# Attention and a low-rank mixer MLP on one core: token tiles in a shared ring of eight, and the preparation of batch 2 moved to the end of batch 0

## The chip, the cores and the metric

The kernel runs on one core of a Trainium2 chip. The metric is device time in microseconds (us) for one execution. PE is the matrix engine, PEld its weight loads; DVE, ACT and POOL are the vector, scalar and GpSimd engines; SP is the queue from which most DMAs are issued. Each engine executes its own instructions in program order and waits on semaphores for the others.

## What is computed

For 8 batches of 12 heads, 448 tokens and head width 64, in fp32 outside and bf16 inside the chip:

```python
q_n, k_n = rmsnorm(q, g_q), rmsnorm(k, g_k)          # over the head width
attn = softmax(q_n @ k_n.T / 8)                      # per head
x = (attn @ v), heads side by side                   # (8, 448, 768)
u = x + (U @ V mixing over the 448 tokens)           # rank 32
out = u + relu(u @ w_ch1) @ w_ch2                    # 768 -> 3072 -> 768
```

## The kernel before

**Units of work.** A batch has three *loads* t of four heads each (t = 0..23) and six *pairs* p of two heads each (p = 0..47). Load 6 and pair 12 are the first of batch 2. For each load, q and k arrive in fp32 by a DMA on SP (`load`, halves s = 0 for k and 1 for q), v by another (`load_v`). The preparation of a load is `squares` (ACT for t < 2 and t > 5, POOL otherwise), `reduce` (DVE), `rsqrt` (two ACT instructions), `scale` (DVE, two multiplies for each of the two pairs), `yield_port` (a 1x1 POOL copy that makes POOL wait for DVE) and `cast_v` (POOL). The squares of loads from 4 on share a single buffer (line 221, `bufs=1`), so the squares of q cannot start before the sums of k have been taken. `transposes` (L250) turns a pair's q and k around on PE for pairs below 14, and by a DMA on SP above; the two copies out of PSUM and, for the DMA form, `gains` are on DVE. Then come `scores` (PE), `expo` (ACT) and `values` (PE, followed by three DVE instructions: L302 the reciprocal, L303 the three whole token tiles, L306 the shared half tile).

**Token tiles.** 448 tokens are 3.5 tiles of 128. An even batch has three whole tiles and a half one, the odd batch after it a half one and three whole ones; the two halves share one tile of 128 rows. Before the change the whole tiles of a batch are one buffer `x3` of a pool of two, and the shared tiles are two constants `xss` that are set to zero at the start (L129 and L130). The second of them is also the operand of `heat` (L759), matmuls at the start whose result nobody reads.

**Order.** The program order is written out by hand. `head` (L591) does batch 0's attention and its low-rank mixing. Then, for each batch b, the matmuls of its MLP (`mlp`, L482) are the filling, and `weave` (L743) puts pieces of other work between them: the attention of batch b+1 and then its mixing. `mlp` yields after every six matmuls; I call these six a *group*. For batch 0 there are 44 groups: 20 of the first layer (L488, hidden blocks 4 to 23) and 24 of the second (L413, six products `po` of four groups each, every one followed by a DVE addition L506 and a store on SP). `weave` spreads items by their weights over a share of the volume: the attention of batch 1 over a share of 0.66 (FA0), the mixing of batch 1 over 0.09 (FM); the last quarter of batch 0 then runs without anything between. An item of weight 0 follows directly on the one before it.

**What is prepared when.** Loads run two ahead: during pairs 8 to 11 SP issues loads 6 and 7, and ACT, DVE and POOL prepare load 6 and half of load 7, so that batch 2's attention finds its first pair ready when batch 1's MLP begins. The second weight, `w2b`, is loaded by six DMAs on POOL's queue: the first ahead of pair 6, one after each of the pairs 6 to 10 (`late`).

**PSUM.** `ps_mm` has three buffers, used in turn by the MLP products, by the transposes, and by some of the values and mixing products; a product can only start when the buffer that it gets has been read out.

Of the kernel before, what the change touches and what calls it, by code (L numbers as in the profile page):

```python
# [17 lines left out]
def kernel(  # L18
# [45 lines left out]
    xpool = ctx.enter_context(tc.tile_pool(name="xpool", bufs=2))  # L64
# [26 lines left out]
    FA, FM, NPE, FA0 = (0.74, 0.77), 0.09, 14, 0.66  # L91
# [20 lines left out]
    def E_of(p):  # L112
        return Es[p % 3 if p < 6 else p % 2]
# [4 lines left out]
    xss = [consts.tile([P, dm], BF16, name=f"xs{i}") for i in range(2)]  # L118

    def setup():  # L120
        nc.scalar.preload_act_table_set("natural_log_exp_and_others")
        make_identity(nc, ident)
        nc.gpsimd.memset(eps, D * 1e-6)
        for t in vas:
            nc.gpsimd.memset(t[:, :, :, D:D + 1], 1.0)
        for t in Es:
            nc.gpsimd.memset(t[:, :, 0:PAD], 0.0)
            nc.gpsimd.memset(t[:, :, PAD + NJ * S:], 0.0)
        for t in xss:  # L129
            nc.gpsimd.memset(t, 0.0)  # L130
        nc.gpsimd.memset(UT, 0.0)
        nc.gpsimd.memset(Vsh, 0.0)
        nc.gpsimd.memset(one, 1.0)
        for i, g in enumerate((g_q, g_k)):
            nc.scalar.dma_start(grow[:, i], g.rearrange("(o a d) -> o a d", o=1, a=1).to_broadcast([1, 2, D]))
# [42 lines left out]

    def load_w2(half, i):
        c, d = slice(8 * i, 8 * (i + 1)), slice(half * HALF, (half + 1) * HALF)  # L180
        nc.gpsimd.dma_start(w2b[:, c, d], w2r[:, c, d])
# [3 lines left out]
    qks, vts, sqs, rstds, qkns, qkTs, scs, x3_of = {}, {}, {}, {}, {}, {}, {}, {}  # L185
# [95 lines left out]
    def values(p, hh):  # L281
        b = p // 6
        par = b % 2
        if b not in x3_of:
            x3_of[b] = xpool.tile([P, 3, dm], BF16, tag="x3", name="x3")
        x3, xs, E, va = x3_of[b], xss[(b // 2) % 2], E_of(p), va_of(p // 2)
        t0, sh, rows = (0, 3, slice(0, 64)) if par == 0 else (1, 0, slice(64, 128))
        hl = 2 * (p % 2) + hh
        d0 = (2 * (p % 6) + hh) * D
        if hh and p < 6:  # L290
            o = ps_mm.tile([P, 4, D + 1], FP32, tag="mm")
        elif hh and p % 6 == 5:
            o = ps_s.tile([P, 4, D + 1], FP32, tag="s", name="o")
        else:
            o = ps_o.tile([P, 4, D + 1], FP32, tag="o")
        for i, off in enumerate(OFFS[par]):
            for kc in range(NJ):
                c = PAD + kc * S + off
                nc.tensor.matmul(o[:, i, :], E[:, hh, c:c + P], va[:, hl, kc, :],  # L299
                                 start=(kc == 0), stop=(kc == NJ - 1))  # L300
        rec = attn.tile([P, 4], FP32, tag="rec")
        nc.vector.reciprocal(rec, o[:, :, D])  # L302
        nc.vector.tensor_tensor(x3[:, :, d0:d0 + D], o[:, t0:t0 + 3, 0:D],  # L303
                                rec[:, t0:t0 + 3].rearrange("p c -> p c ()").to_broadcast([P, 3, D]),
                                OP.mult)
        nc.vector.tensor_tensor(xs[rows, d0:d0 + D], o[rows, sh, 0:D],  # L306
                                rec[rows, sh:sh + 1].to_broadcast([64, D]), OP.mult)
# [4 lines left out]
    def x_tiles(b):  # L312
        xs = xss[(b // 2) % 2]
        full = [x3_of[b][:, i, :] for i in range(3)]
        return full + [xs] if b % 2 == 0 else [xs] + full
# [200 lines left out]
    def attention(b, extra={}):  # L516
# [3 lines left out]
        def add(weight, fn, *args):  # L520
            items.append((weight, lambda: fn(*args)))
# [9 lines left out]
        for p in range(b * 6, b * 6 + 6):  # L531
# [10 lines left out]
            if not odd and p > 7 and t + 2 < NT:  # L542
                add(0, load, t + 2, 1, (0,))
# [15 lines left out]
            if odd and p > 6 and 6 <= t + 2 < NT:  # L559
                add(0, load, t + 2, 1, (1,))  # L560
# [22 lines left out]
            if odd and p > 6 and 6 <= t + 2 < NT:  # L583
                add(0, load_v, t + 2)
            if p in extra:
                add(0, *extra[p])
        add(2, values, b * 6 + 5, 0)
# [128 lines left out]
    scratch = consts.tile([1, 1], BF16, name="scratch")  # L716

    def yield_port(t, pr):

        nc.gpsimd.tensor_copy(scratch, qkns[2 * t + pr][0:1, 1, 0, 0, 0:1])  # L720

# [33 lines left out]
    def heat(n):  # L755
        if n:
            warm = ps_mm.tile([P, 512], FP32, tag="mm")
            for _ in range(n):
                nc.tensor.matmul(warm, xss[1][:, 0:P], xss[1][:, 0:512], start=True, stop=True)  # L759
# [5 lines left out]
    with tc.manual_schedule():  # L765
        head()
        late = {6 + i: (load_w2, *divmod(i + 1, 3)) for i in range(5)}
        for b in range(B):
            fill, total = mlp(b), volume(b)
            if b + 1 < B:  # L770
                rest = [(4, lambda: (load_w2(0, 0), transposes(6), reduce(4, ALL, (0,))))] + attention(1, late)
                weave(fill, total * (FA[b % 2] if b else FA0), attention(b + 1) if b else rest)
                weave(fill, total * FM, mixing(b + 1))
            for _ in fill:
                pass
# [30 lines left out]
```

The softmax here doesn't subtract the row's maximum and nothing guards it: scores larger than these inputs give would overflow.

## Time and profile before

| | us |
|---|---|
| median of 4 runs | 580.17 (578.74 to 580.99) |
| the profiled execution | 579.44 |
| its span, first to last instruction | 577.7 |
| PE busy | 560.3 (97%) |
| DVE busy | 396.6 (69%) |
| ACT busy | 279.9 (48%) |
| POOL busy | 77.6 (13%) |
| DVE L303, three whole tiles, 128x192, 96 times | 34.3 busy, 0.357 each |
| DVE L306, the half tile, 64x64, 96 times | 20.8 busy, 0.217 each |

An engine's busy time is the union of its instructions' spans. PE at 97% does the work that sets the end almost everywhere; so the places of interest are those where PE stands still, and the instructions whose movement can open or close such a place. A wait in a timeline stands in square brackets behind the instruction that waited: how long its engine was idle and what ended it.

### The profile page before, as it was taken

The numbers are of one execution on the slowest core, as the hardware profiler recorded it, in microseconds if no ns is written. First come the engines' busy times: TensorE is split into PE (matmuls) and PEld (weight loads), VectorE is DVE, ScalarE is ACT, GpSimd is POOL, SyncE is SP. The second block draws the span as 40 slices with busy tenths as digits, with TensorE's granted clock in tenths as the row PEclk, the third lists the DMA queues.
The fourth block names the chain that finished last, engine by engine and source line by source line (L and its number), as shares of the span: only waits on it lengthen the run. The fifth ranks groups of instructions, "written<-read, shape, count | busy, mean of one in ns | idle before, by whom it ended". The sixth has DMA issues, their size and how long they took to land.

```text
span 577.7 us, 11342 instructions
## 1 busy us (share of the span) xinstructions
PE 560.3 (97%) x4590; PEld 306.1 (53%) x4613; DVE 396.6 (69%) x811; ACT 279.9 (48%) x413; POOL 77.6 (13%) x122
## 2 busy tenths in 40 slices
PE   7799999999999999999999999999999999999997
PEld 2365556544565555544465555544456555554464
DVE  5878987399875787747776598747767487453342
ACT  4956662266721775166641676246661376302200
POOL 4751421000020000000020000000001000000010
PEclk9999999999999999999999999999999999999999
DMA  8999997524463455444525454456234541040021
GB/s 211 232 241 237 234 172 163 125 56 91 115 133 97 116 131 129 107 104 112 129 74 117 106 128 113 121 143 129 64 84 130 131 97 33 29 110 0 1 54 56
DMA packets 103648, 67.22 MB, mean 116 GB/s; under 512 B 54716, under 2 KB 102060, under 8 KB 103596
## 3 DMA queue, kind: packets, MB, share of 16 engines
q1 hardware_dynamic: 93988, 56.77, 41.6%
q0 software_dynamic: 9376, 9.44, 10.0%
q8 instruction: 36, 0.59, 0.4%
q10 hardware_dynamic: 232, 0.30, 0.2%
q14 instruction: 16, 0.13, 0.1%
HBM read 52.19 MB, written 11.01 MB: 109 GB/s over the span
## 4 chain that ended last, share of the span: by engine, by line
PE 86%; DVE 7%; ACT 3%; DMA 2%; issue 1%; POOL 1%; DVEq 0%; POOLq 0%; ACTq 0%
PE ph L488 35%; PE pb L413 10%; PE po L413 8%; PE o L299 7%; PE pe L413 7%; PE sc L273 7%; PE pa L413 6%; ACT E L278 2%; DVE qkn L244 2%; PE pu L337 2%; PE warm L759 1%; DMA qkT<-qkn 1%; DVE rstd L231 1%; PE first L732 1%; DVE hT L404 1%
## 5 line engine op out<-in xcount | busy, mean ns | idle before, releaser
L488 PE MATMUL ph<-u,w1b 128*128 128x384 bf16 (+1 forms) x1107 | 231.0, 353 | 1.4
L278 ACT ACTIVATE E<-sc 112x896 bf16<-112x896 f32 x184 | 159.9, 914 | 58.0 <-PE sc L273 57.1
L488 PEld LDWEIGHTS <-w1b 128*128 128x128 bf16 x1128 | 102.8, 98 | 108.6 <-issue 22.4
L413 PEld LDWEIGHTS <-hT 128*128 128x128 bf16 x1080 | 101.3, 98 | 71.5 <-issue 9.2
L491 ACT ACTIVATE hT<-ph 128x384 bf16<-128x384 f32 (+1 forms) x95 | 51.4, 543 | 136.2 <-PE ph L488 134.4
L493 DVE TENSOR_SCALAR hT<-ph 128x512 bf16<-128x512 f32 (+1 forms) x93 | 57.8, 622 | 53.6 <-PE ph L488 52.9
L299 PEld LDWEIGHTS <-E 112*128 112x128 bf16 x1472 | 58.5, 98 | 15.9 <-DVE xs L306 1.6
L244 DVE TENSOR_TENSOR qkn<-qk,rstd 112x512 bf16<-112x512 f32 x84 | 56.2, 706 | 7.9 <-ACT rstd L237 4.1
L299 PE MATMUL o<-va,E 112*128 112x65 bf16 x1440 | 61.0, 194 | 0.5 <-DVE xs L306 0.5
L273 PE MATMUL sc<-qkT 64*128 64x448 bf16 x384 | 55.5, 355 | 3.5 <-ACT E L278 1.4
L413 PE MATMUL po<-w2b,hT 128*128 128x384 bf16 x288 | 52.5, 326 | 0.6 <-DVE hT L493 0.6
L231 DVE TENSOR_REDUCE rstd<-sq 112x16 f32<-112x1024 f32 x40 | 48.5, 1212 | 4.8 <-ACT sq L223 4.1
L720 POOL COPY scratch<-qkn 1x1 bf16<-1x1 bf16 x44 | 10.3, 234 | 307.7 <-DVE qkn L244 306.0
L413 PE MATMUL pa<-w2b,hT 128*128 128x384 bf16 x264 | 49.5, 326 | 0.0
L413 PE MATMUL pb<-Tw,hT 128*128 128x384 bf16 x264 | 48.0, 326 | 0.0
L223 ACT ACTIVATE sq<-qk 112x1024 f32<-112x1024 f32 x36 | 38.2, 1062 | 2.3 <-issue 1.1
L303 DVE TENSOR_TENSOR x<-o,rec 128x192 bf16<-128x192 f32 x96 | 34.3, 357 | 3.7
L448 POOL TENSOR_TENSOR o<-o,x 128x384 f32<-128x384 f32 x11 | 12.6, 1144 | 161.1 <-DVE o L447 161.1
L302 DVE RECIPROCAL rec<-o 128x4 f32<-128x4 f32 x96 | 17.0, 177 | 23.6 <-PE o L299 23.3
L273 PEld LDWEIGHTS <-qkT 64*128 64x128 bf16 x384 | 12.5, 94 | 34.9 <-issue 30.9
L428 ACT ACTIVATE pb<-pa 128x384 f32<-128x384 f32 x11 | 5.2, 475 | 50.1 <-PE pa L413 50.1
L339 DVE TENSOR_TENSOR x<-pu,x 128x768 bf16<-128x768 f32 (+1 forms) x27 | 23.2, 864 | 7.2 <-PE pu L337 7.0
(106 smaller groups left out, 449.9 us busy)
## 6 DMA issues: line engine op xcount, KB each, us to landing
qk<-in_k_dram SPq DMA_DIRECT2D x21, 448.0 KB, 5.0
vt<-in_v_dram SPq DMA_DIRECT2D x20, 448.0 KB, 4.7
qk<-in_q_dram SPq DMA_DIRECT2D x19, 448.0 KB, 3.9
w2b<-in_moe_w_ch_dram POOLq DMA_DIRECT2D x6, 768.0 KB, 12.7
w1b<-in_moe_w_ch_dram POOLq DMA_DIRECT2D x2, 1536.0 KB, 22.0
out_dram<-o SPq DMA_DIRECT2D x15, 168.0 KB, 2.5
out_dram<-o SPq DMA_DIRECT2D x16, 144.0 KB, 2.1
out_dram<-o SPq DMA_DIRECT2D x15, 120.0 KB, 2.1
```

Of the source, the lines that this page charges most:

```text
L223: nc.scalar.activation(sqs[t, s][:, hs], qks[t, s][:, hs], AF.Square)
L231: nc.vector.tensor_reduce(rstds[t][:, s, hs].rearrange("p h j -> p (h j)"), sqs[t, s][:, hs].rearrange("p h (j d) -> p (h j) d", d=D), AX, ...
L244: nc.vector.tensor_tensor(qkn[:, s].rearrange("p j h d -> p h j d"), qks[t, s][:, hp].rearrange("p h (j d) -> p h j d", d=D), rstd[:, s, h ...
L273: nc.tensor.matmul(sc[:, hh, 0:S], kT[pp, kc * SP:kc * SP + P], qT[pp, :], start=True, stop=True)
L278: nc.scalar.activation(E_of(p)[:, :, PAD + kc * S:PAD + (kc + 1) * S], scs.pop((p, kc))[0:SP, :, 0:S], AF.Exp, scale=float(D) ** 0.5)
L299: nc.tensor.matmul(o[:, i, :], E[:, hh, c:c + P], va[:, hl, kc, :], start=(kc == 0), stop=(kc == NJ - 1))
L303: nc.vector.tensor_tensor(x3[:, :, d0:d0 + D], o[:, t0:t0 + 3, 0:D], rec[:, t0:t0 + 3].rearrange("p c -> p c ()").to_broadcast([P, 3, D]), ...
L339: nc.vector.tensor_add(xv, pu[rows, 0:n, 0:HALF], xv)
L413: nc.tensor.matmul(ps, lhs[:, c, :], rhs[:, c, :], start=first and c == 0, stop=last and c == NC - 1, skip_group_check=again)
L488: nc.tensor.matmul(ph, w1b[:, dc, hc * P:(hc + 1) * P], u[:, dc, :], start=(dc == 0), stop=(dc == KD - 1))
L491: nc.scalar.activation(hT[:, hc, 0:n], ph, AF.Relu)
L493: nc.vector.tensor_relu(hT[:, hc, 0:n], ph)
```

## The change

Three things change together.

First, the token tiles. `x3` and `xss` are replaced by one constant `ring` of eight tiles of 128 x 768. The first pair of batches uses slots 1, 2, 3 for the even batch, 5, 6, 7 for the odd one and slot 4 for the shared tile; the next pair uses slot 0 for the shared tile, and so on in turn. The slots of an even batch, the shared one included, now lie side by side, so its values are scaled by one DVE instruction of 128x256 in place of one of 128x192 and one of 64x64. (The lower half of the shared tile then holds finite numbers of no meaning until the odd batch writes its own there; the mixing multiplies them by zero.) For every second even batch the four products are put into PSUM in a rotated order. An odd batch keeps two instructions, the half tile first. `heat` reads slot 0, and slot 0 is set to zero before slot 4.

Second, the loads. In the attention of batch 1, loads run one ahead instead of two: loads 6 (k; then q and v) are written into pairs 10 and 11, load 7's k at the end of pair 11, and load 7's q and v behind everything else. The w2b DMAs go out in twos after pairs 6 and 7 and singly after pair 8.

Third, the preparation. Everything that prepares batch 2 is taken out of the attention of batch 1 and collected in `later`: 16 items, in this order: squares and sums of load 6's k, squares and sums of its q, rsqrt, scale for pair 12, a POOL copy, squares of load 7's k, scale for pair 13, a POOL copy, cast of v, transposes of pair 12, gains (empty here), sums of load 7's k, load 7's q, load 7's v. They are woven, with equal weights, into a share of 0.2 (FL) of batch 0's volume behind the mixing of batch 1.

```diff
     attn = ctx.enter_context(tc.tile_pool(name="attn", bufs=2))
-    xpool = ctx.enter_context(tc.tile_pool(name="xpool", bufs=2))
     upool = ctx.enter_context(tc.tile_pool(name="upool", bufs=1))
...
     NWARM, NH = 16, 2
-    FA, FM, NPE, FA0 = (0.74, 0.77), 0.09, 14, 0.66
+    FA, FM, NPE, FA0, FL = (0.74, 0.77), 0.09, 14, 0.66, 0.2
     flat = Tw.rearrange("p f c n -> p (f c n)")
...
-    xss = [consts.tile([P, dm], BF16, name=f"xs{i}") for i in range(2)]
+    ring = consts.tile([P, 8, dm], BF16, name="ring")
+    SHARED = (4, 0)
+    cold = ring[:, 0, :]
...
             nc.gpsimd.memset(t[:, :, PAD + NJ * S:], 0.0)
-        for t in xss:
-            nc.gpsimd.memset(t, 0.0)
+        nc.gpsimd.memset(cold, 0.0)
+        nc.gpsimd.memset(ring[:, 4, :], 0.0)
         nc.gpsimd.memset(UT, 0.0)
...
+    def load_w2s(i0, i1):
+        for i in range(i0, i1):
+            load_w2(*divmod(i, 3))
     def load_w2(half, i):
...
     NT, NP = B * 3, B * 6
-    qks, vts, sqs, rstds, qkns, qkTs, scs, x3_of = {}, {}, {}, {}, {}, {}, {}, {}
+    qks, vts, sqs, rstds, qkns, qkTs, scs, pts = {}, {}, {}, {}, {}, {}, {}, {}
...
-    def values(p, hh):
+    outs = {}
+    def weigh(p, hh):
         b = p // 6
-        par = b % 2
-        if b not in x3_of:
-            x3_of[b] = xpool.tile([P, 3, dm], BF16, tag="x3", name="x3")
-        x3, xs, E, va = x3_of[b], xss[(b // 2) % 2], E_of(p), va_of(p // 2)
-        t0, sh, rows = (0, 3, slice(0, 64)) if par == 0 else (1, 0, slice(64, 128))
+        par, g = b % 2, b // 2 % 2
+        E, va = E_of(p), va_of(p // 2)
         hl = 2 * (p % 2) + hh
-        d0 = (2 * (p % 6) + hh) * D
         if hh and p < 6:
...
         for i, off in enumerate(OFFS[par]):
+            n = (i + 1) % 4 if par == 0 and g else i
             for kc in range(NJ):
                 c = PAD + kc * S + off
-                nc.tensor.matmul(o[:, i, :], E[:, hh, c:c + P], va[:, hl, kc, :],
+                nc.tensor.matmul(o[:, n, :], E[:, hh, c:c + P], va[:, hl, kc, :],
                                  start=(kc == 0), stop=(kc == NJ - 1))
+        outs[p, hh] = o
+    def normalise(p, hh):
+        b, o = p // 6, outs.pop((p, hh))
+        par, g = b % 2, b // 2 % 2
+        d0 = (2 * (p % 6) + hh) * D
         rec = attn.tile([P, 4], FP32, tag="rec")
         nc.vector.reciprocal(rec, o[:, :, D])
-        nc.vector.tensor_tensor(x3[:, :, d0:d0 + D], o[:, t0:t0 + 3, 0:D],
-                                rec[:, t0:t0 + 3].rearrange("p c -> p c ()").to_broadcast([P, 3, D]),
+        if par == 0:
+            t0, t1, rows, r0 = 0, 4, slice(0, P), 1 - g
+        else:
+            t0, t1, rows, r0 = 1, 4, slice(0, P), 5
+            nc.vector.tensor_tensor(ring[64:128, SHARED[g], d0:d0 + D], o[64:128, 0, 0:D],
+                                    rec[64:128, 0:1].to_broadcast([64, D]), OP.mult)
+        nc.vector.tensor_tensor(ring[:, r0:r0 + t1 - t0, d0:d0 + D], o[:, t0:t1, 0:D],
+                                rec[:, t0:t1].rearrange("p c -> p c ()").to_broadcast([P, t1 - t0, D]),
                                 OP.mult)
-        nc.vector.tensor_tensor(xs[rows, d0:d0 + D], o[rows, sh, 0:D],
-                                rec[rows, sh:sh + 1].to_broadcast([64, D]), OP.mult)
+    def values(p, hh):
+        weigh(p, hh)
+        normalise(p, hh)
...
     def x_tiles(b):
-        xs = xss[(b // 2) % 2]
-        full = [x3_of[b][:, i, :] for i in range(3)]
-        return full + [xs] if b % 2 == 0 else [xs] + full
+        g = b // 2 % 2
+        return [ring[:, n, :] for n in ((1, 2, 3, SHARED[g]) if b % 2 == 0 else (SHARED[g], 5, 6, 7))]
...
-    def attention(b, extra={}):
+    scratch = consts.tile([1, 1], BF16, name="scratch")
+    def yield_port(t, pr):
+        nc.gpsimd.tensor_copy(scratch, qkns[2 * t + pr][0:1, 1, 0, 0, 0:1])
+    ahead = {cast_v: 6, squares: 6, reduce: 6, rsqrt: 6, scale: 6, yield_port: 6,
+             transposes: 12, gains: 12}
+    def attention(b, extra={}, later=None):
...
         def add(weight, fn, *args):
-            items.append((weight, lambda: fn(*args)))
+            put = items if later is None or args[0] < ahead.get(fn, NP) else later
+            put.append((weight, lambda: fn(*args)))
+        def late_add(fn, *args):
+            later.append((0, lambda: fn(*args)))
...
             sums(p, 0)
-            if not odd and p > 7 and t + 2 < NT:
-                add(0, load, t + 2, 1, (0,))
+            lead = 1 if b == 1 else 2
+            if not odd and p > 9 and t + lead < NT:
+                add(0, load, t + lead, 1, (0,))
             if not odd and more:
...
                 add(0, cast_v, t + 1)
-            if odd and p > 6 and 6 <= t + 2 < NT:
-                add(0, load, t + 2, 1, (1,))
+            if odd and 6 <= t + lead < NT:
+                add(0, load, t + lead, 1, (1,))
             add(1, scores, p, (2, 3))
...
                 add(0, reduce, t + 2, ALL, (0,))
-            if odd and p > 6 and 6 <= t + 2 < NT:
-                add(0, load_v, t + 2)
+            if odd and 6 <= t + lead < NT:
+                add(0, load_v, t + lead)
             if p in extra:
                 add(0, *extra[p])
+            if p == 11:
+                add(0, load, 7, 1, (0,))
+                late_add(load, 7, 1, (1,))
+                late_add(load_v, 7)
         add(2, values, b * 6 + 5, 0)
...
-    scratch = consts.tile([1, 1], BF16, name="scratch")
-    def yield_port(t, pr):
-        nc.gpsimd.tensor_copy(scratch, qkns[2 * t + pr][0:1, 1, 0, 0, 0:1])
     firsts = {}
...
             for _ in range(n):
-                nc.tensor.matmul(warm, xss[1][:, 0:P], xss[1][:, 0:512], start=True, stop=True)
+                nc.tensor.matmul(warm, cold[:, 0:P], cold[:, 0:512], start=True, stop=True)
...
         head()
-        late = {6 + i: (load_w2, *divmod(i + 1, 3)) for i in range(5)}
+        late = {6: (load_w2s, 1, 3), 7: (load_w2s, 3, 5), 8: (load_w2s, 5, 6)}
         for b in range(B):
...
             if b + 1 < B:
-                rest = [(4, lambda: (load_w2(0, 0), transposes(6), reduce(4, ALL, (0,))))] + attention(1, late)
+                later = []
+                rest = [(4, lambda: (load_w2(0, 0), transposes(6), reduce(4, ALL, (0,))))] + attention(1, late, later)
                 weave(fill, total * (FA[b % 2] if b else FA0), attention(b + 1) if b else rest)
                 weave(fill, total * FM, mixing(b + 1))
+                if b == 0:
+                    weave(fill, total * FL, [(1, piece) for _, piece in later])
             for _ in fill:
...
```

## Prediction

> **What bounds the kernel now.** I read the page first, then the chain, the busy times by stage, and the timelines of the stages that the change touches.
>
> ```profile
> span 577.7 us, 11342 instructions
> ...
> PE 560.3 (97%) x4590; PEld 306.1 (53%) x4613; DVE 396.6 (69%) x811; ACT 279.9 (48%) x413; POOL 77.6 (13%) x122
> ...
> PE 86%; DVE 7%; ACT 3%; DMA 2%; issue 1%; POOL 1%; DVEq 0%; POOLq 0%; ACTq 0%
> ```
>
> PE is the bound: 97% busy, 86% of the chain that ended last. The change leaves the number and shapes of the useful matmuls alone, so it can only win where PE stands still, and lose where it opens a new hole. By stage (stage, length, then busy times and counts, PE first, DVE third, ACT fourth):
>
> ```profile
> 15.00:43.00 28.00, 23.66 (x335) 14.60 (x336) 22.94 (x66) 20.66 (x28) 18.00 (x20) 1.00 1.15 236
> ...
> 46.00:75.00 29.00, 28.57 (x264) 16.39 (x263) 26.46 (x52) 20.99 (x35) 9.96 (x11) 1.00 1.15 226
> 75.00:85.00 10.00, 9.29 (x108) 5.75 (x107) 7.90 (x18) 5.80 (x9) 1.94 (x3) 1.00 1.20 204
> 85.00:101.00 16.00, 16.00 (x162) 9.65 (x159) 11.90 (x28) 5.42 (x7) 2.20 (x4) 1.00 0.73 149
> 101.00:111.00 10.00, 10.00 (x63) 5.99 (x62) 2.90 (x4) 0.00 (x0) 0.00 (x0) 1.00 0.55 119
> ...
> 115.00:155.00 40.00, 39.64 (x300) 18.62 (x303) 38.12 (x76) 26.71 (x39) 2.81 (x6) 1.00 0.42 96
> ```
>
> From 46 to 111 us (batch 0's MLP with batch 1's attention) PE is idle 0.43 + 0.71 + 0 + 0 = 1.14 us in all. That is the most that a better placement can give there. From 101 to 111 DVE works 2.9 us and ACT not at all: that is where the preparation goes. In the head PE idles, but the work there is tied to four engines and the loads.
>
> **Part 1: what leaves pairs 9 to 11.** The largest hole in PE from 46 to 111 us:
>
> ```profile
> 78.20 1.22 DVE L231 TENSOR_REDUCE rstd<-sq 112x16 f32<-112x1024 f32 x1
> ...
> 79.11 0.33 PE L337 MATMUL pu<-t4b,Vsh 128*128 128x384 bf16 x1
> ...
> 79.45 0.56 DVE L493 TENSOR_SCALAR hT<-ph 128x384 bf16<-128x384 f32 x1
> 79.45 1.06 ACT L223 ACTIVATE sq<-qk 112x1024 f32<-112x1024 f32 x1
> 80.06 1.14 PE L413 MATMUL po<-w2b,hT 128*128 128x384 bf16 x6 [0.62 <-DVE hT L493]
> ```
>
> The sum at 78.20 is that of load 6's k, by its place in the written order (end of pair 9). The relu of the last hidden block stands behind it on DVE and starts at 79.45, though its product was over at 78.7; PE's first product of the second layer waits for it until 80.06. The sum moves, the relu starts 0.7 us sooner, the hole of 0.62 us closes, with about 0.1 us of weight loads behind it: **-0.7 us**. The other sums, multiplies and copies taken from 82 to 94 us hide beside a PE that has no idle time from 85 to 101: nothing. The eight PE transposes of pair 12 (0.41 us of PE) only move.
>
> **Part 2: where they go.** The 16 items share 0.2 of 44 groups: 8.8 groups, 0.55 group each, behind group 34. So load 6's k is squared after group 35, its sum stands after group 36, pair 12's scale after 38, its transposes (item 12, due at 6.6) after group 41. Engines run ahead of PE, but DVE takes its instructions in order, and group 36 ends with an eviction of `po` that stands ahead of that first sum:
>
> ```profile
> 103.23 0.56 DVE L506 TENSOR_TENSOR o<-po,x 128x384 f32<-128x384 f32 x1 [0.45 <-PE po L413]
> ...
> 107.13 0.56 DVE L506 TENSOR_TENSOR o<-po,x 128x384 f32<-128x384 f32 x1 [3.34 <-PE po L413]
> 110.67 1.12 PEld L488 LDWEIGHTS <-w1b 128*128 128x128 bf16 x6
> ```
>
> These evictions end groups 36 and 40, and 110.67 is batch 1's first product. From 103.23, with durations of the same forms: eviction, next start after 0.50; sum of k 1.21; squares of q 1.06 on ACT, which must wait for that sum since both use one buffer (the rows above show it: sum until 79.42, squares from 79.45); sum of q 1.21; the two rsqrt instructions 0.61 (46.84 to 47.45); the first multiply 0.69, the second 0.60 later. With 0.03 us at each of four changes of engine the first multiply ends at 108.6, the second at 109.2. Group 41 ends three groups of 0.975 us before batch 1's first matmul at 110.83, so at 107.9. PE is in order: the transposes need the multiplies, so it stands 0.7 us, does four of eight, stands again, and leaves at 109.45 rather than at 107.9 + 0.41 = 108.3: **+1.15 us**. Queued behind them on PE are groups 42 to 44 and all of batch 1. Bounds: 0, if the sum of k came before the eviction of group 36; 5.0, if it came only after that of group 40 (3.9 us later). I take the order as written.
>
> Behind this, DVE does pair 13's scale, eviction 40, the copies and the sum of load 7's k, all before the scores of pair 12 (112.22 before) need them. Load 7's q is on SP behind the store of eviction 40. It goes out at about 111 in place of 89.6 and, at the 3.8 us from issue to landing of the load at 112.5, lands near 115. ACT wants it at 114.4 (behind the two exps after 112.82). ACT waits 0 to 1.5 us; behind its squares stand a relu and two exps. PE has three product buffers and only every second relu is ACT's, so I take **+0.1**, bounds 0 and 1.
>
> **Part 3: loads.** SP isn't paced by PE and waits only for buffers and stores. Load 6's k still goes out at 60.7; its q and v come behind the first store (87.7) and land, by the 8.2 and 7.8 us that loads took at 89.6 and 91.5, by 97, ahead of their squares. The w2b DMAs take POOL 0.94 us each. The third goes out some 4 us sooner, but pushes the squares of load 5's k from 58.20 to 59.15; their sum isn't taken until 63.7, so this hides. Before, the third landed 14.6 us after 62.5 and the sixth 9.5 us after 87.7, both 2 to 4 us before PE's need (about 81 and 99.6): PE never waited for w2b, so loading it sooner gives 0. Bounds -0.1 to +0.4: multiplies of pair 9 may meet the shifted squares.
>
> **Part 4: the ring.** One multiply of 256 columns replaces 192 and 64 for 48 heads. In the head the two start 0.28 apart and the next instruction 0.13 later, 0.41 together; 128 more columns cost 0.15, so 256 take 0.355: 0.055 saved per head of an even batch, 2.6 us of DVE in all. It counts only where DVE is on PE's path: two heads at 24.7 to 25.9 and a wait at 38.2, **-0.2**; between 115 and 155 DVE is busy 38.1 of 40 us, but PE idles only 0.36, so -0.1 at most per even batch, **-0.1** taken.
>
> The heat starts after one memset rather than two:
>
> ```profile
> 2.34 1.42 POOL L130 MEMSET xs<- 128x768 bf16 x2
> ...
> 3.81 6.09 PE L759 MATMUL warm<-xs 128*128 128x512 bf16 x16 [3.81 <-POOL xs L130]
> ...
> 10.14 0.57 PE L257 MATMUL pt<-ident,qkn 112*128 112x112 bf16 x8
> ...
> 15.91 1.89 POOL L225 TENSOR_TENSOR w2b<-hT 112x1024 f32<-112x1024 f32 x1 [0.16 <-DMA hT<-in_q_dram]
> ...
> 16.90 1.45 DVE L244 TENSOR_TENSOR qkn<-qk,rstd 112x512 bf16<-112x512 f32 x1 [0.80 <-ACT rstd L237]
> ```
>
> The chain runs from the heat to pair 0's transposes, whose operand was ready at 8.8, so 0.7 us come free at 10.1 and last to the multiply at 16.90. That takes 1.45 us instead of the 0.68 of its twin at 18.27, and ends 0.55 after POOL's squares (15.91 to 17.80), whose start is set by a DMA. Moved to 16.2 it still meets them. So I let the 0.7 end there: **0**, bound -0.7.
>
> [...]
>
> [...]
>
> **Sum.** -0.7 + 1.15 + 0.1 + 0 - 0.2 - 0.1 + 0 = +0.25 us on the profiled execution's 579.44 (span 577.7 and 1.7 around it), so 579.7. The median of the runs shown is 0.73 above that execution; on it the forecast is 580.4. I take about 0.3% (1.7 us) as what a measurement of this kernel can tell from no change.
>
> **Rivals.**
> *Slower: the chain to pair 12.* Place: DVE's order between the evictions of groups 36 and 40. If the sums slip behind the eviction of group 40 (rotation of buffers or the cuts of the weave one place later than I count), pair 12's transposes are ready 3.9 us later, and the stall is 5.0: 580.4 + 3.9 = 584.3. A partial slip, with 1 us from the wait for load 7's q, gives about 582.5. It decides from a chain 1.7 us longer. For it: DVE is idle 3.3 us before that eviction, so each slip is paid in full. Against it: the order as written.
> *Faster: nothing stalls and the head's 0.7 carries.* 580.4 - 1.15 - 0.7 = 578.5; against it: the dependence of the squares on one buffer. With the remaining 0.4 of PE's holes from 46 to 75 it is 578.1.
> *The move does nothing* (PE waits at 80 for something else and the chain hides): 580.17 - 0.2 = 580.0, inside the forecast.
>
> **Numbers.** Forecast (with the third rival) 0.60, 579.2 to 581.6; slower rival 0.22, mostly beyond 0.3%; faster rival 0.18, about half of it there, with a remainder for the unknown costs in the head. Same by the 0.3% mark 0.62; slower 0.21; faster 0.17. The range reaches from the faster rival (578.1) to the partial slower one with the noise of the runs (1 us either way): 578.0 to 583.0.
>
> **What would show it.** No wait before the first `po`; PE waiting for DVE's multiply ahead of pair 12's transposes by about 1 us; ACT waiting for a DMA at its first squares of batch 1's MLP; pair 0's transposes near 9.4 but the head's end barely moved. Wrong if PE goes through group 41 without a wait, or if holes appear between 115 and 155.

## The result and the profile after

The changed kernel takes 581.99 us (median of 48 runs, 577.38 to 586.0) against 579.94 us for the kernel before on the same chips (72 runs): ratio 1.0031, interval 1.0019 to 1.0043. The forecast was 580.4 us within 578.0 to 583.0. So the range holds, the size does not: +2.05 us instead of +0.25. Three of the prediction's terms were measured close to their sizes; three others, each of about 1 us or more, were missing from its sum or far from their sizes.

Part of the 2 us goes with the granted clock of PE, which differs from run to run. Where it was 0.998 or more over the whole run, the changed kernel takes 580.5 us (median of 15 of its 48 runs) and the kernel before 579.4 (60 of the 109 runs that the experiments below compare with): 1.1 us apart. Of the runs of the changed kernel 19 of 58 had that clock (e7's ten included), of the kernel before 60 of 109, of the seven other kernels below with the moved preparation 44 of 84; whether the change makes the lower clock likelier is open.

The profiled execution took 582.33 us. Its span is 580.5 us. First the page, the busy time of each engine:

```profile
PE 561.4 (97%) x4590; PEld 306.5 (53%) x4613; DVE 390.5 (67%) x763; ACT 280.2 (48%) x413; POOL 77.5 (13%) x122
```

DVE has 48 instructions and 6.1 us less, PE is no less busy, and the span is longer: what DVE saves does not show in the span. Next the busy times by stage (stage, length, then PE, PEld, DVE, ACT, POOL):

```profile
46.00:75.00 29.00, 26.59 (x239) 15.24 (x238) 25.61 (x48) 19.08 (x32) 11.21 (x13) 1.00 1.20 223
75.00:85.00 10.00, 9.46 (x109) 5.88 (x109) 7.02 (x20) 4.43 (x6) 2.01 (x3) 1.00 1.08 168
...
101.00:111.00 10.00, 9.36 (x60) 5.40 (x57) 7.30 (x9) 2.56 (x4) 0.00 (x0) 1.00 0.54 118
```

PE now idles 2.41 us between 46 and 75 (0.43 before), 0.54 between 75 and 85 (0.71 before), and 0.64 between 101 and 111 (0 before). These windows stand still while the work of this trace comes 1.2 us later: 0.58 us of the 2.41 are a wait of the head that lay ahead of 46 before. To see what persists, I take the starts of the exponentials of the pairs (four each, two to a half) as milestones, in two traces of the changed kernel (the second is run e7 below), each against the profile of before:

| from, to | trace 1 | trace 2 | the prediction's term |
|---|---|---|---|
| start to pair 6 | +1.21 | +4.07 | -0.2 and 0 |
| pair 6 to pair 9 | +1.28 | +1.27 | 0 (bounds -0.1 to +0.4) |
| pair 9 to pair 10 | +0.35 | +0.36 | none |
| pair 10, first half | -0.53 | -0.53 | -0.7 |
| pair 10, second half, to pair 11, second half | +0.07 | +0.06 | none |
| pair 11, second half, to pair 12 | +1.16 | +1.16 | +1.15 |
| pair 12 to the last half of pair 47 | -1.62 | -1.65 | -0.1 and +0.1 |
| from there to the end | +0.96 | +1.19 | none |

Without the first row the two add up to +1.7 and +1.9 us. That is near the difference of the medians, but the two do not measure the same: the medians hold the heads with their lower clocks as well. The first row is dealt with at e7 and e8.

**What was foreseen.** The chain to pair 12, in the timeline of the changed kernel:

```profile
105.16 0.56 DVE L526 TENSOR_TENSOR o<-po,ring 128x384 f32<-128x384 f32 x1 [0.45 <-PE po L433]
105.63 1.21 DVE L236 TENSOR_REDUCE rstd<-sq 112x16 f32<-112x1024 f32 x1
106.88 1.06 ACT L228 ACTIVATE sq<-qk 112x1024 f32<-112x1024 f32 x1 [6.23 <-DVE rstd L236]
107.97 1.22 DVE L236 TENSOR_REDUCE rstd<-sq 112x16 f32<-112x1024 f32 x1 [1.12 <-ACT sq L228]
...
109.89 2.50 DVE L249 TENSOR_TENSOR qkn<-qk,rstd 112x512 bf16<-112x512 f32 x4 [0.70 <-ACT rstd L242]
110.64 0.37 PE L262 MATMUL pt<-ident,qkn 112*128 112x112 bf16 x4 [0.64 <-DVE qkn L249]
111.24 0.37 PE L262 MATMUL pt<-ident,qkn 112*128 112x112 bf16 x4 [0.23 <-DVE qkn L249]
```

Each line waits for the one above it (the two rsqrt instructions, 109.22 to 109.80, are left out), and PE stands at the end of the row twice, 0.64 and 0.23 us. The hole before the first second-layer product is closed: the relu no longer stands behind a sum but waits for its own product (0.75 us of an idle DVE), and the first `po` follows without a wait in brackets:

```profile
81.76 0.56 DVE L513 TENSOR_SCALAR hT<-ph 128x384 bf16<-128x384 f32 x1 [0.75 <-PE ph L508]
...
82.37 1.14 PE L433 MATMUL po<-w2b,hT 128*128 128x384 bf16 x6
```

**What was not.** The squares of load 5's k on POOL and the two multiplies of pair 9 on DVE, in the kernel before:

```profile
58.20 1.91 POOL L225 TENSOR_TENSOR sq<-qk 112x1024 f32<-112x1024 f32 x1
...
59.04 2.23 DVE L244 TENSOR_TENSOR qkn<-qk,rstd 112x512 bf16<-112x512 f32 x2
```

and POOL, DVE and PE between 58 and 65 us in the changed one:

```profile
58.71 1.82 POOL L186 DMA_DIRECT2D w2b<-in_moe_w_ch_dram  x2
...
60.54 1.91 POOL L230 TENSOR_TENSOR sq<-qk 112x1024 f32<-112x1024 f32 x1
60.64 2.97 DVE L249 TENSOR_TENSOR qkn<-qk,rstd 112x512 bf16<-112x512 f32 x2
...
63.54 0.44 DVE L263 TENSOR_SCALAR qkT<-pt,gg 128x448 bf16<-128x448 bf16 x1
...
64.33 1.15 PE L508 MATMUL ph<-u,w1b 128*128 128x384 bf16 x6 [0.84 <-DVE qkT L264]
```

Two w2b DMAs hold POOL for 1.82 us; the squares come out 0.10 us ahead of the multiplies instead of 0.84, and these take 2.97 us for two instead of 2.23 (1.28 where no squares meet them, e9). Behind them on DVE stand the copies of pair 8 out of PSUM, and PE waits 0.84 us for the product buffer that they read. Last, the end, between batch 6's MLP and batch 7's:

```profile
518.16 5.12 PE L508 MATMUL ph<-u,w1b 128*128 128x512 bf16 x22 [1.02 <-DMA u<-ring]
```

PE stands 1.02 us for the last DMA transpose of batch 7's tokens, issued at 513.82, where before it did not wait at all (this product then started at 515.26).

### The profile page after: what moved, and what is told of

Read it like the earlier page. It is cut to its first block, busy times and chain, and to the rows that moved or that the text cites. A ratio compares the mean times of both kernels' runs of the same rounds, so it can differ in the third digit from the quotient of the medians.

```text
span 580.5 us, 11296 instructions
## 1 busy us (share of the span) xinstructions
PE 561.4 (97%) x4590; PEld 306.5 (53%) x4613; DVE 390.5 (67%) x763; ACT 280.2 (48%) x413; POOL 77.5 (13%) x122
## 4 chain that ended last, share of the span: by engine, by line
PE 88%; DVE 6%; ACT 2%; DMA 1%; issue 1%; POOL 0%; DVEq 0%; POOLq 0%; ACTq 0%
PE ph L508 36%; PE pb L433 10%; PE o L304 8%; PE pe L433 7%; PE po L433 7%; PE sc L278 7%; PE pa L433 7%; DVE qkn L249 2%; PE pu L357 2%; DVE rstd L236 1%; ACT E L283 1%; PE warm L791 1%; DMA u<-ring 1%; PE first L764 1%; DVE ring L359 1%
## 5 line engine op out<-in xcount | busy, mean ns | idle before, releaser
L249 DVE TENSOR_TENSOR qkn<-qk,rstd 112x512 bf16<-112x512 f32 x84 | 57.7, 727 | 7.8 <-ACT rstd L242 4.4
L359 DVE TENSOR_TENSOR ring<-pu,ring 128x768 bf16<-128x768 f32 (+3 forms) x36 | 31.0, 864 | 14.4 <-PE pu L357 13.8
L321 DVE TENSOR_TENSOR ring<-o,rec 128x256 bf16<-128x256 f32 (+1 forms) x96 | 37.5, 391 | 2.4
L468 POOL TENSOR_TENSOR o<-o,ring 128x384 f32<-128x384 f32 x11 | 12.6, 1144 | 161.6 <-DVE o L467 161.6
```

The source lines that it names most:

```text
L249: nc.vector.tensor_tensor(qkn[:, s].rearrange("p j h d -> p h j d"), qks[t, s][:, hp].rearrange("p h (j d) -> p h j d", d=D), rstd[:, s, h ...
L321: nc.vector.tensor_tensor(ring[:, r0:r0 + t1 - t0, d0:d0 + D], o[:, t0:t1, 0:D], rec[:, t0:t1].rearrange("p c -> p c ()").to_broadcast([P, ...
L359: nc.vector.tensor_add(xv, pu[rows, 0:n, 0:HALF], xv)
```

## The experiments

Every kernel was compared with the kernel before on the same chip; the interval of a ratio is some 0.2% to either side, so verdicts on single stretches rest on the traces.

### The moved part and the ring apart: e1 to e4

e1 is the changed kernel with the w2b DMAs issued singly again:

```diff
-        late = {6: (load_w2s, 1, 3), 7: (load_w2s, 3, 5), 8: (load_w2s, 5, 6)}
+        late = {6 + i: (load_w2s, i + 1, i + 2) for i in range(5)}
```

> The changed kernel, but the second-weight DMAs go out one after each of pairs 6 to 10, as before. My theory: in the profile after the change POOL's squares of load 5's k, pushed behind two DMA issues, start at 60.54 and hold up the multiplies for pair 9 (60.64, 2.97 us for two in place of 2.23), and PE stands 0.84 us at 63.3; the exps of pair 7 lose 1.4 us there. So the multiplies come back to about 2.2 us, that hole closes and the time falls by 1.4 us against the changed kernel: ratio to before about 1.0007. Rival (the changed kernel lost by chance of the loads' landings in the head, or by the chain to pair 12 alone): the ratio stays near 1.003.

Measured: 580.4 us, ratio 1.0015 (0.9997 to 1.0033). Pair 6 to pair 9 costs +0.40 instead of +1.28, so 0.9 us come back there and not the 1.4 expected; the kernel before, run again unaltered, has +0.32 in this stretch (e8). The two multiplies take 2.10 us; pair 12's +1.16 and the end's +1.27 stay.

e2 is the ring alone: loads, preparation and w2b DMAs as before the change.

```diff
-            lead = 1 if b == 1 else 2
-            if not odd and p > 9 and t + lead < NT:
+            lead = 2
+            if not odd and p > 7 and t + lead < NT:
...
-                rest = [(4, lambda: (load_w2(0, 0), transposes(6), reduce(4, ALL, (0,))))] + attention(1, late, later)
+                rest = [(4, lambda: (load_w2(0, 0), transposes(6), reduce(4, ALL, (0,))))] + attention(1, late)
...
-                if b == 0:
-                    weave(fill, total * FL, [(1, piece) for _, piece in later])
```

> The ring of eight alone: loads, second-weight DMAs and the preparation of batch 2 stand as before the change. My theory: the ring only gains: 0.1 to 0.2 us in the head and the 1.6 us that the profile after the change shows in the three later odd attentions, so ratio 0.997. Rival: the 1.2 us that the changed kernel loses before pair 4 come from the ring (heat sooner, other instructions on DVE) and not from the chance of when v lands, so the exps of pair 4 stand about 1.2 us later than before and the ratio is 0.999 to 1.000.

Measured: 577.92 us, ratio 0.9977 (0.9959 to 0.9994): faster than before. Pair 11 to 12 is back at 0.00, the end costs +0.03, and pair 12 to 47 gains 1.66 us. The ring, for which the prediction had -0.3 in all, is the part that gains.

e3 puts pair 12's transposes and gains last of the sixteen late items, and e4 does that with the DMAs singly as well:

```diff
                 if b == 0:
+                    later = later[:11] + later[13:] + later[11:13]
                     weave(fill, total * FL, [(1, piece) for _, piece in later])
```

> The changed kernel, but pair 12's transposes and gains are the last of the 16 late items (after group 43 and not 41). My theory: the chain through the one buffer of squares ends about 1.15 us after PE reaches the transposes, and two more groups of PE work (1.95 us) cover that: no wait of PE for DVE's multiply there, 1.15 us less than the changed kernel, ratio 1.0011. Rival: the copies of the transposes now end too late for the scores of pair 12 and the wait only moves into batch 1: ratio 1.003.

> Both edits: second-weight DMAs singly and pair 12's transposes last. If the two costs are separate they add: 2.5 us less than the changed kernel, ratio 0.9988. Rival: if both were one delay seen twice, or chance, the ratio is that of the better of the two alone, 1.001 or more.

Measured: e3 578.76 us, ratio 0.9979 (0.9959 to 0.9999); e4 579.57 us, ratio 0.9988 (0.9968 to 1.0007). In both, pair 11 to 12 costs -0.05: the whole +1.16 is the place of the transposes against their chain. But pair 6 to 9 costs -0.15 in e3, which has the DMAs in twos: there load 5's k landed only at 60.60, the squares waited for it until 60.74 and the multiplies (from 59.73) were nearly through. So DMAs in twos alone don't decide; e9 takes that up. e4 comes to the ratio that was expected, but not by the expected sum: there, too, load 5's k was late (the squares start at 60.47, pair 6 to 9 costs -0.14), and the end costs +1.34.

### A code fetch at the end, the order in the ring, and chance: e5 to e8

In the traces with a long wait at the end, an 8 KB packet of the queue that the profile calls q14 instruction fell beside the last transposes (at 516.8 us in trace 1, at 497.6 in the kernel before). I take it for a fetch of code, by that name. e5 is e3 with 24 instructions on DVE at the start that do nothing of use:

```diff
+        for _ in range(24):
+            nc.vector.memset(idle, 0.0)
         make_identity(nc, ident)
```

> The changed kernel with pair 12's transposes last of the sixteen, and 24 one-element memsets on DVE at the start, where DVE has nothing to do until the first loads land. They do no work; they shift where in DVE's instruction stream the 8 KB code fetches fall. Theory (the loss of about 1 us behind pair 47 comes from a code fetch that meets the last DMA transposes of the tokens): the fetch at about 514 us moves to some other place, PE's wait for the last transpose before batch 7's MLP (1.3 us with pair 12's transposes last, 0.2 before the change) shrinks to 0.2 to 0.4, and the time is 577.5 us, ratio 0.996. Rival (the wait comes from how the ring's tiles are read or from the stores in front of it on SP): the wait stays at 1.0 to 1.4 us, 578.7, ratio 0.998.

Measured: 579.1 us, ratio 0.998 (0.9956 to 1.0004). The fetch moved from 513.5 to 498.5 us, and PE's wait shrank from 1.25 to 0.34 us. The stretch costs +0.28 in place of +1.18, so 0.9 us of it goes with the place of the fetch. The total did not reach 577.5 because pair 6 to 9 was +1.29 again, and the head +1.7 (below); why 0.3 us remain is open.

e6 is e2 with the two instructions of the odd batches in the old order, three whole tiles first, then the half one:

```diff
-            nc.vector.tensor_tensor(ring[64:128, SHARED[g], d0:d0 + D], o[64:128, 0, 0:D],
-                                    rec[64:128, 0:1].to_broadcast([64, D]), OP.mult)
         nc.vector.tensor_tensor(ring[:, r0:r0 + t1 - t0, d0:d0 + D], o[:, t0:t1, 0:D],
                                 rec[:, t0:t1].rearrange("p c -> p c ()").to_broadcast([P, t1 - t0, D]),
                                 OP.mult)
+        if par:
+            nc.vector.tensor_tensor(ring[64:128, SHARED[g], d0:d0 + D], o[64:128, 0, 0:D],
+                                    rec[64:128, 0:1].to_broadcast([64, D]), OP.mult)
```

> The ring alone, loads and preparation as before the change, and in the odd batches the three whole tiles are scaled first and the half tile after them, as before the change. Theory (the ring's gain of 1.6 us between pairs 18 and 47 comes from the order of the two instructions in odd batches): that stretch is as before the change again, within 0.3 us, and the time is 579.4 us, ratio 0.9995. Rival (the gain comes from the ring itself, a tile being free for writing as soon as its own readers are done): the gain of 1.6 us stays, 577.9, ratio 0.9977.

Measured: 579.57 us, ratio 0.9985 (0.9964 to 1.0006). Between the starts of pair 18 and of the last half of pair 47 it gains 0.30 us, where e2 gains 1.63: some 1.3 us of the ring's gain is this order, the theory's side. (The medians of e2 and e6 can't tell, as their intervals overlap.) One odd head of batch 3, changed kernel:

```profile
232.59 0.17 DVE L314 RECIPROCAL rec<-o 128x4 f32<-128x4 f32 x1
232.80 0.23 DVE L319 TENSOR_TENSOR ring<-o,rec 64x64 bf16<-64x64 f32 x1
233.04 0.36 DVE L321 TENSOR_TENSOR ring<-o,rec 128x192 bf16<-128x192 f32 x1
233.31 1.21 DVE L236 TENSOR_REDUCE rstd<-sq 112x16 f32<-112x1024 f32 x1
```

and the same head in e6:

```profile
228.94 0.18 DVE L314 RECIPROCAL rec<-o 128x4 f32<-128x4 f32 x1
229.15 0.36 DVE L319 TENSOR_TENSOR ring<-o,rec 128x192 bf16<-128x192 f32 x1
229.52 0.23 DVE L323 TENSOR_TENSOR ring<-o,rec 64x64 bf16<-64x64 f32 x1
229.78 1.22 DVE L236 TENSOR_REDUCE rstd<-sq 112x16 f32<-112x1024 f32 x1
229.81 0.69 PE L304 MATMUL o<-va,E 112*128 112x65 bf16 x16 [0.27 <-DVE ring L323]
```

The same four instructions take 0.72 us from the first start to the last in one order and 0.84 in the other. With the half tile second it starts 0.37 behind the large one, and the sum 0.26 behind it; with the half tile first the large one starts 0.24 behind it and the sum only 0.27 behind a 0.36 us instruction. From the reciprocal to the end of the two multiplies both orders take 0.81 us, so within the row the PSUM buffer is free no sooner. What comes sooner is the reciprocal: it starts 0.25 us behind the instruction ahead of it on DVE (`gains`, from 232.34) in the changed kernel, and 0.37 behind it in e6 (from 228.57). PE's wait of 0.27 us for that buffer is gone (its next product starts at 233.46 without one). Why the starts depend on the order no trace shows; the lines give the price alone: from the start of `gains` to PE's next product 1.12 us in the changed kernel and 1.24 in e6.

> The changed kernel once more, unaltered, for a second trace. What comes from the order of the instructions must return: pair 11 to 12 longer by 1.15 us, the hole before the first second-layer product gone, PE's wait of about 1.0 us for the last transposes of batch 7. What came from the moment at which a load landed may differ: the stretch from pair 6 to pair 9 is 1.3 us longer again if the w2b DMAs in twos cause it (theory of the first runs), and 0 to 0.5 us longer if the collision of the squares with the multiplies of pair 9 is a matter of when load 5's k lands.

Measured (e7, the changed kernel unaltered): 581.95 us, ratio 1.0024 (0.9999 to 1.0048). Its trace is the second column of the table: from pair 6 on, the same losses and gains to within 0.1 us, but for the end's 0.2.

> The kernel before once more, unaltered, for a second trace: it shows how far the start of pair 4, of pair 9 and of pair 12 differ between two executions of one kernel. If the head's 0.2 to 1.0 us seen so far are chance, pair 4 starts at 29.9 to 30.5; if they belong to the change, within 0.1 us of 29.91.

Measured (e8, the kernel before unaltered): 580.24 us. Pair 4 starts 0.30 us later than in the first profile, pair 6 0.74, pair 9 1.06, pair 12 1.06. The 0.32 between pairs 6 and 9 is a collision without any change: load 5's k landed later, the squares start 0.48 us ahead of the multiplies, these take 2.55, and PE waits 0.43. In the head, part of it goes with the clock: from 24 to 32 us the granted PE clock was

| | before | e8 | after | e7 | e5 | the other nine |
|---|---|---|---|---|---|---|
| clock, 24 to 32 us | 1.00 | 0.79 | 0.79 | 0.50 | 0.71 | 1.00 |
| start of pair 6 against before, us | 0 | +0.74 | +1.21 | +4.07 | +1.73 | -1.38 to +0.31 |

So the head's +1.2 and +4.1 can't be put down to the change, as the kernel before shows a lower clock too; without it the ring's heads run from -1.4 to +0.3.

### The collision, the sum of the repairs, the one buffer: e9 to e12

e9 is the changed kernel with the w2b DMAs, still in twos, behind the squares on POOL's queue:

```diff
             if odd and more2:
                 add(0, squares, t + 2, ALL, (0,))
+            if p - 1 in extra:
+                add(0, *extra[p - 1])
...
-            if p in extra:
-                add(0, *extra[p])
```

> The changed kernel, with the w2b DMAs still in twos, but on POOL's queue behind the squares of the next pair instead of ahead of them. Theory (the two DMAs, 1.82 us of POOL, push the squares of load 5's k from 0.8 us ahead of the multiplies of pair 9 to 0.1 us ahead, so that both multiplies are held until the squares end): the squares start about 1.8 us sooner, the two multiplies take 1.3 to 1.4 us together instead of 2.97, PE's wait of 0.84 us for pair 9's product is gone, and the stretch from pair 6 to pair 9 is -0.1 to +0.3 us against before instead of +1.28; the time is 580.8 us, ratio 1.001. If load 5's k lands late, the squares start late all the same and the wait can be up to 0.6 us. Rival (the wait belongs to the moved loads, since k's landing and the sums set it): +1.3 us as in the changed kernel, 582, ratio 1.003. Pair 12's wait of 1.15 us and the wait for the last transposes stay under both.

Measured: 579.61 us, ratio 1.0003 (0.9982 to 1.0024). Its timeline shows the theory's order:

```profile
57.51 1.88 POOL L230 TENSOR_TENSOR sq<-qk 112x1024 f32<-112x1024 f32 x1
...
59.43 1.28 DVE L249 TENSOR_TENSOR qkn<-qk,rstd 112x512 bf16<-112x512 f32 x2
```

The squares are over at 59.39 (the two w2b DMAs follow, from 59.34), the multiplies take 1.28, pair 6 to 9 costs -0.15, and pair 12's +1.17 stays. The wait of 0.84 us is the place of the two DMAs in POOL's queue. It shows in three of the four traces that have them ahead of the squares (trace 1, e5, e7: squares 0.10 us ahead of the multiplies in each). The fourth is e3, where the late k kept POOL from starting. e10 and e12 below have e9's order but a late k (squares from 60.09 and 59.45, behind the starts of both multiplies), so it is e9's trace that shows it. One part of the expectation failed: the loss at the end did not stay. It is -0.14 here, PE does not wait for the last transpose, and the 8 KB packet begins 2.75 us after the transpose's issue (2.95 in trace 1), in a kernel with the changed kernel's count of instructions.

e10 has the three repairs together: DMAs behind the squares, pair 12's transposes last, 24 memsets. e11 is e2 once more on the same chip.

> The three places mended together: w2b DMAs behind the squares, pair 12's transposes last of the sixteen, 24 one-element memsets on DVE at the start that shift the code fetches. Theory: nothing is left of the losses of 1.28, 1.16 and 0.9 us; what remains is the gain of 0.5 us at the first second-layer product and of 1.5 us behind pair 18: 578.0 us, ratio 0.9965, and faster than the ring alone by 0.3 us or more. Rival (each place mended opens another, the padding by moving a fetch to somewhere that counts): no better than the ring alone, ratio 0.998.

> The ring alone once more, as the measure for the best version. The gain of 1.6 us between pairs 18 and 47 must return; 578.5 us, ratio 0.9975. The squares and the multiplies of pair 9 may meet (2.98 us for the two, PE waiting 0.6) or not (1.3 to 2.2), by when load 5's k lands.

Measured: e10 577.87 us, ratio 0.997 (0.9949 to 0.999); e11 577.86 us, ratio 0.9962 (0.9939 to 0.9986). Both beat the kernel before and the changed one, and neither the other. All three losses are gone from e10's trace, with 0.13 us left at the end. The theory's lead of 0.3 us over the ring alone is less than the intervals can tell; from pair 6 to the end the traces stand at -1.7 (e10), -1.5 (e2) and -1.2 (e11) against the kernel before. In e11 the squares met the multiplies (2.79 us, PE waiting 0.44), as the expectation allowed, and PE waited 0.55 for the last transpose.

e12 leaves pair 12's transposes where the change put them, on top of e9, and gives the squares of load 6's q a buffer of their own (one that load 5 has left):

```diff
-                sqs[t, s] = early[0:SP, t, s] if t < 4 else norm.tile([SP, HG, NJ * D], FP32, tag="sq", name="sq", bufs=1)
+                sqs[t, s] = early[0:SP, t, s] if t < 4 else k1 if (t, s) == (6, 1) else norm.tile([SP, HG, NJ * D], FP32, tag="sq", name="sq", bufs=1)
```

> The kernel with the w2b DMAs behind the squares (e9), and the squares of load 6's q in a second buffer, so that they need not wait for the sums of k; pair 12's transposes stay where the change put them. Theory (the one buffer is the link that makes the chain too long): the two sums follow each other behind the eviction of group 36 without ACT's squares between, so sum of k 103.0 to 104.2, sum of q to 105.4, rsqrt to 106.05, the first multiply to 106.8, the second to 107.4, where PE comes to the transposes at 107.4: PE's two waits (0.64 and 0.23 us) shrink to 0.1 together at most, the stretch from pair 11's second half to pair 12 is 0 to +0.1 against before in place of +1.17, and the time is 578.5 us, ratio 0.998. Rival (the chain is bound by DVE's place behind the evictions, the buffer counts for nothing since ACT is free): 0.8 us or more of wait remain, ratio 1.000.

Measured: 579.8 us, ratio 0.999 (0.9969 to 1.0011). The profiled execution is faster than that (span 575.2; its head is the fastest of all), and its timeline is:

```profile
101.62 1.21 DVE L236 TENSOR_REDUCE rstd<-sq 112x16 f32<-112x1024 f32 x1
102.74 1.21 DVE L236 TENSOR_REDUCE rstd<-Tw 112x16 f32<-112x1024 f32 x1
...
105.82 0.56 PE L262 MATMUL pt<-ident,qkn 112*128 112x112 bf16 x8
```

The second sum starts 1.12 us behind the first instead of 2.34, PE does all eight transposes without a wait, and pair 11 to 12 costs -0.05: the link is the one buffer, as the prediction said. The stall is thus mended in two ways, e3's and this one; the medians of e12 and e9 (ratios 0.999 and 1.0003) are too close to show it. The end costs +0.92 again.

## Why the prediction was right or wrong

**Part 1, the hole at 80 us, -0.7: right in kind, 0.2 too large.** The relu starts when its product is done and PE no longer waits. The stretch gained 0.53 us: gap 0.62 to 0.09. Of this the ring alone gives 0.25 (e2). The extra 0.1 of weight loads that I added was not there, and 0.09 us of gap stays.

**Part 2, the stall before pair 12, +1.15: right, +1.16 in both traces.** The order of the chain, the two pieces of the stall and its cause (e3, e4: the place; e12: the one buffer of the squares) came as worked out. The slower rival, a slip behind the eviction of group 40, did not happen: the sum stands directly behind that of group 36. Load 7's q, +0.1: ACT waited for it, 0.36 us in trace 1 and 0.96 in e7, but PE did not; pair 12's two halves are as far apart as before.

**Part 3, loads and w2b, 0: wrong, +1.28.** The step that failed is "pushes the squares of load 5's k from 58.20 to 59.15; their sum isn't taken until 63.7, so this hides". I priced the shift by who waits for the squares' result and not by what runs beside them. In both kernels the first multiply is held until the squares are over and ends 0.56 us after them, and the second takes 0.68; with the squares 0.74 us later against the multiplies, the first takes 2.37 us instead of 1.63. The prediction's own row at 16.90 had this price: a multiply that ends 0.55 us after POOL's squares. PE's product buffer hangs on the copies behind the multiplies. The bound of +0.4 named that collision but left out the queue behind it on DVE. That 0.84 of the 1.28 is one wait, and a further 0.25 one at a later product (67.85, the copies again), is read from trace 1; e9, where only the DMAs' place differs, has neither. The rest is not traced to a cause. (PE's wait for ACT among pair 6's scores is 0.74 us in the nine traces with the moved preparation and 0.25 in the five without; e9 has it too and still comes to -0.15.)

**Not considered: the cuts of the weave, +0.35.** Items taken out of pairs 9 to 11 carry half a weight with them (the transposes of pair 12), so all cuts move by a fraction of a group. At pair 9 two multiplies (from 76.70 and 77.30) now come ahead of a relu:

```profile
76.70 0.68 DVE L249 TENSOR_TENSOR qkn<-qk,rstd 112x512 bf16<-112x512 f32 x1
...
77.90 0.55 DVE L513 TENSOR_SCALAR hT<-ph 128x384 bf16<-128x384 f32 x1
...
78.51 1.14 PE L508 MATMUL ph<-u,w1b 128*128 128x384 bf16 x6 [0.45 <-DVE hT L513]
```

Every kernel here with the moved preparation has this gap of 0.45, the kernels without it do not. That the half weight is the cause is argued from the order, not tried. It eats most of part 1's gain.

**Part 4, the ring, -0.3: wrong, about -1.6 behind pair 12.** The head's term can't be told from the clock. Even batches came as priced: 0.61 us to 0.55 for one head from the reciprocal to the next instruction, and e6, which has the ring without the new order, gains 0.3 us from pair 18 on. Missing was a term for odd batches: the prediction took the two instructions that an odd batch keeps as no change, though their order was turned, and that is 1.3 us over batches 3, 5 and 7 (e6). In batch 1 it narrows the hole ahead of the first `po` as well (0.62 in e6, 0.37 in e2). The heat starts 0.68 us sooner and pair 0's transposes 0.84 (9.30 in place of 10.14), and the gain is gone by pair 2 (-0.10 in trace 1), as taken.

**Not considered: the end, about +1.0.** Some 0.9 us of it, in trace 1 and e7, goes with a code fetch in the stretch of the last transposes (e5 moves it away). It is no fixed price of the change: e9, with the same count of instructions, doesn't have it, the packet being 0.2 us earlier there. That the change brought the fetch near by the mere count of its instructions is argued: 24 idle ones suffice to move it. It could equally have moved one away.

The faster rival failed on the stall, which came; "does nothing" is excluded by the table. The forecast lay near the truth because some -1.5 of ring stood against +1.28, +0.35 and +1.0, none of them in the sum: a balance of errors, and so luck. What the prediction understood is the stall before pair 12 and most of the hole at 80 us.

## What to carry to other kernels

Price a shifted instruction by what it will run beside, and then follow the queue behind whatever it slows: 0.95 us on POOL's queue, hidden by its own consumer, cost PE 0.84 through a DVE multiply and a PSUM buffer. Read a reordering of two adjacent instructions as a change of its own, with the starts of the row as price; 0.12 us per head was worth more here than merging two instructions. When a change of many parts moves the time little, run the parts alone first: here the ring alone (0.9977 and 0.9962) is all of the gain that the medians show.

## What the runs showed of the hardware

- **A code fetch beside a DMA transpose went with a late end of it.** The last transpose of batch 7 has 16 increments of its semaphore in the traces; in trace 1 the sixteenth came at 518.12 and PE started at 518.16, in the kernel before at 515.22 and 515.26. In four traces (trace 1, e3, e7, e12) fifteen came within 0.2 us and the sixteenth 0.85 to 0.9 us after them, and in these an 8 KB packet of q14 began 2.9 to 3.2 us after the issue. With a packet at 1.9, 2.2, 2.8, 3.5 or 4.6 us, or with none near (ten traces in all), the sixteen came within 0.2 us. e5 moved the packet and the lag went; how a fetch delays the last increment no trace shows. In e1, e4 and e11 PE waited for another reason: SP's two stores ahead of the transpose took 2.0 to 2.1 us instead of 1.0, for which the traces show no cause: a 16 KB packet of q8 instruction starts while they are issued, but so it does in traces without the delay.
- **POOL and DVE together.** Squares of 1.9 us on POOL and the two multiplies: 1.28 us for the two when apart (e9, e12), and also when the squares start during the second (e3, e4, e10); 2.10 to 2.23 when the squares are 0.8 to 1.0 us ahead, 2.55 at 0.48 (e8), 2.79 at 0.25 (e11), 2.97 at 0.10; 2.98 when the first multiply is ahead and the squares start during it (e2). In the traces in which a multiply meets squares that already run, it ends 0.55 to 0.56 us after them, as the one at 16.90 did in the kernel before (0.55) and the same one, from 16.45, in trace 1 (0.55).
- **The head's granted clock differs between executions of one kernel**: 1.00 and 0.79 from 24 to 32 us in two traces of the kernel before, 0.79 and 0.50 in two of the changed one. One trace of a head can't price a term of 0.7 us there.
